# The last row of wo in two column parts, y copied 640 to 384, stores awaited on GpSimd, and wq loaded in 4, 2 and 2 blocks

## The chip, the cores and the metric

One core of a Trainium2 chip. The metric is device time in microseconds (us) of one execution; most executions of a kernel agree within 0.3%. "Fast" and "slow" are states of the chip. Ratios are the mean time of one kernel's fast runs over the mean of the other's fast runs of the same rounds, so they are not quite the ratio of the medians that are quoted beside them.

## The reference

Attention of four new tokens for each of 32 sequences over a cache of 2048 keys, with a projection ahead of it and one behind:

```python
B, Sq, D = 32, 4, 1024
Hq, Hkv, Sk, Dh = 32, 4, 2048, 128           # all arrays bf16
q = (x @ wq).reshape(B, Sq, Hq, Dh).transpose(0, 2, 1, 3)
k, v = repeat(k_cache, 8, axis=1), repeat(v_cache, 8, axis=1)
p = softmax(einsum("bhqd,bhkd->bhqk", q, k) * Dh ** -0.5)
y = einsum("bhqk,bhkd->bhqd", p, v).transpose(0, 2, 1, 3).reshape(B, Sq, Hq * Dh) @ wo
```

The k and v caches are 2 MB each for each sequence, wq and wo 8 MB each: 151 MB to be read.

## The kernel before

`big` in SBUF has eight slots of 2 MB. Slots 0 to 3 hold wq at first and v later (so the first four v loads wait for the projection, "qproj"); slots 4 to 6 hold k in turn. A k load waits until the transposes of the k that was in its slot three sequences earlier are done on VectorE (DVE). All loads go through one queue, issued by SyncE (SP) in program order.

```python
LEAD, S1, S2, VS, KS = 3, 6, 12, 4, 3
NC = D // 2
WO = (4, 4, 4, 4, 4, 4, 2, 2, 2, 1, 1)        # rows of wo (256 KB each) in each load
...
for c in range(4):                            # wq: four loads of 2 MB
    p.dma("sp", lambda e, c=c: e.dma_start(w_sb[:, 2*c:2*c+2, :], wq_v[:, 2*c:2*c+2, :]), [], ("wq", c), f"s_w{c}")

loads = [("k", b) for b in range(LEAD)]       # order: k0 k1 k2, v0 k3, v1 k4, v2 k5, ...
for b in range(B):
    ahead = b + LEAD + (b >= S2)
    ks = [("k", a) for a in range(len(loads) - b, ahead + 1) if a < B]
    loads += [("v", b)] + ks if b < S1 else ks + [("v", b)]
for kind, b in loads:
    waits = ["qproj"] * (b < VS) if kind == "v" else []
    if kind == "v" and b >= VS: waits = [("pv", b - VS)]
    if kind == "k" and b >= KS: waits = [("kt", b - KS, 1)]
    ...                                       # p.dma("sp", ... 2 MB into its slot)
...                                           # the loads of wo, in the pieces of WO
for kt in range(KT):                          # projection: 64 matmuls of 512 columns
    ... p.op("pe", mm, ["xT_evac", ("wq", kt // 2)], ...)
...
pe_idle(3, ring[0], xT_flat[:, 0:512], [("qs", 4)])   # keeps TensorE (PE) busy, then the transposes of q
...
def oproj(c):                                 # y = o @ wo, two matmuls of 512 columns for each row
    for h in range(sum(WO[:c]), sum(WO[:c + 1])):
        for j in range(2):
            ... p.op("pe", mm, [("wo", c), ("ot", B - 1)], ("op", j) if h == Hq - 1 else None)

def oproj_out():
    p.op("act", lambda e: e.activation(y_sb[:, 0:NC], ps_s[:, 0:NC], ACT.Copy), [("op", 0)], ("oe", 0))
    p.op("dve", lambda e: e.tensor_copy(y_sb[:, NC:D], ps_s[:, NC:D]), [("op", 1)], ("oe", 1))
    for j, eng in enumerate(("act", "sp")):   # each half is stored from its own queue
        p.dma(eng, ..., [("oe", j)], ("out", j), f"s_o{j}")
...
p.op("sp", lambda e: None, [("out", j) for j in range(2)])    # SP waits for both stores
```

## Time and profile before

| | before |
|---|---|
| median time, range (6 runs) | 363.35 us, 363.28 to 363.69 |
| span of the profiled run | 361.8 us (time 363.62) |
| read from HBM | 151.26 MB |
| first wo matmul that the end hangs on | 356.91 us |
| last landing of wo | 358.13 us |
| last landing of a store | 361.38 us |

How to read it: the span is the time from the first to the last instruction in the trace; the time of the execution is some 1.8 us longer. The lines of the profile that matter are shown and read in the prediction below, with the views they come from. "Landing" is the time at which a DMA engine reports its share of a load as done. A load is shared by 16 engines, so it has 16 landings, and what waits for the load waits for the last of them. The difference between the first and the last of the 16 is called the spread here.

### The profile page before, as it was taken

To read this page: it belongs to the slowest core of one execution; us is meant where nothing else is said; L and a number is where in the kernel's file an instruction comes from. 1 tells how busy PE (TensorE), PEld (TensorE's weight loads), DVE (VectorE), ACT (ScalarE), POOL (GpSimd) and SP (SyncE) were. 2 spreads that over 40 slices of the span, in tenths; PEclk is the share of its full clock that TensorE was granted. 3 is DMA by queue.
4 is the path that set the end of the run, shared out by engine and by line. 5 is a ranking of instruction groups with operands and counts; after the bars stand their busy time and mean duration, and the time that the engine had idled before them with its cause. 6 is when DMAs were issued, how large, how long until landed. Compare 5 with 4: busy or idle time off the path is not lost. (4 is left out here: it accounts for less than half of the span.)

```text
span 361.8 us, 6213 instructions
## 1 busy us (share of the span) xinstructions
PE 307.2 (85%) x3002; PEld 146.8 (41%) x2338; DVE 269.1 (74%) x170; ACT 102.8 (28%) x110; POOL 165.3 (46%) x262
## 2 busy tenths in 40 slices
PE   1988788999989999988999888888888889889896
PEld 1002000454444554444444444444333344449711
DVE  0018799999899888879998888888888888856500
ACT  1014222333333333333333333333322223333000
POOL 8002055355555555554455444445555554444000
PEclk9999999999999999999999999999999999999999
DMA  8999999999999999999999999999999999999995
GB/s 322 431 435 429 431 426 424 431 428 426 423 426 431 426 433 424 430 427 429 431 422 433 428 429 422 431 429 427 431 422 433 429 429 426 427 433 429 408 417 195
DMA packets 11819, 151.66 MB, mean 419 GB/s; under 512 B 1312, under 2 KB 1568, under 8 KB 2336
## 3 DMA queue, kind: packets, MB, share of 16 engines
q1 hardware_dynamic: 11664, 151.39, 98.7%
q8 instruction: 6, 0.10, 0.1%
q10 hardware_dynamic: 144, 0.13, 0.1%
q14 instruction: 5, 0.04, 0.0%
HBM read 151.26 MB, written 0.26 MB: 419 GB/s over the span
## 5 line engine op out<-in xcount | busy, mean ns | idle before, releaser
L325 DVE STREAM_TRANSPOSE KT_sb<-big 128x2048 f32<-128x2048 f32 x64 | 146.6, 2293 | 16.7 <-DMA big<-in_k_cache_dram 16.7
L351 ACT ACTIVATE P_sb<-ps_s,negmx 128x2048 bf16<-128x2048 f32 x32 | 82.1, 2565 | 185.0 <-DVE negmx L347 185.0
L16 PE MATMUL ps_s<-KT_sb,QD_sb 128*128 128x512 bf16 x384 | 103.7, 377 | 0.0
L382 POOL COPY PD_sb<-PT_sb 32x1024 f32<-32x1024 f32 x62 | 64.1, 1034 | 63.4 <-PE ps_r L391 60.5
L382 POOL COPY big<-PT_sb 32x1024 f32<-32x1024 f32 x61 | 63.0, 1034 | 59.1 <-PE ps_r L391 56.4
L347 DVE TENSOR_REDUCE negmx<-ps_s 128x1 f32<-128x2048 f32 x32 | 73.2, 2287 | 12.4 <-PE ps_s L16 11.0
L391 PE MATMUL ps_r<-big 128*128 128x128 bf16 x1024 | 59.8, 219 | 11.3 <-PEq L85 11.3
L391 PE MATMUL ps_r<-big,PD_sb 128*128 128x128 bf16 x1024 | 59.8, 219 | 9.9 <-PEq L85 9.9
L391 PEld LDWEIGHTS ps_r<-big 128*128 128x128 bf16 x1024 | 57.9, 98 | 22.1 <-issue 21.6
L391 PEld LDWEIGHTS ps_r<-big,PD_sb 128*128 128x128 bf16 x1024 | 58.0, 98 | 21.1 <-issue 20.6
L338 PE MATMUL ps_s<-KT_sb,QD_sb 128*128 128x512 bf16 x128 | 48.3, 377 | 18.4 <-PEq L85 18.4
L338 PEld LDWEIGHTS ps_s<-KT_sb,QD_sb 128*128 128x128 bf16 x128 | 12.4, 97 | 103.1 <-issue 103.1
L360 DVE STREAM_TRANSPOSE PT_sb<-P_sb 128x1024 f32<-128x1024 f32 x32 | 39.8, 1245 | 15.8 <-ACT P_sb L351 15.8
L315 POOL COPY QD_sb<-QT_sb 32x64 f32<-32x64 f32 x128 | 29.4, 229 | 46.2 <-DVE QT_sb L294 20.5
L16 PE MATMUL ps_r<-ident 128*128 128x384 bf16 x173 | 33.3, 325 | 0.0
L363 PEld LDWEIGHTS ps_r<-ssum,permf 128*128 128x128 f32 x64 | 11.9, 187 | 24.8 <-issue 23.1
L400 ACT ACTIVATE QT_sb<-ps_r,rinv 128x128 bf16<-128x128 f32 x32 | 11.7, 367 | 29.5 <-PE ps_r L391 27.3
L276 DVE TENSOR_SCALAR KT_sb<-ps_r 128x512 bf16<-128x512 f32 x2 | 1.3, 686 | 20.2 <-PE ps_r L260 20.2
L417 PE MATMUL ps_s<-big,KT_sb 128*128 128x512 bf16 x32 | 12.2, 380 | 2.2 <-DMA big<-in_wo_dram 1.4
L426 DVE CAST P_sb<-ps_s 128x512 bf16<-128x512 f32 x1 | 0.7, 692 | 16.1 <-PE ps_s L16 16.1
L16 PE MATMUL ps_s<-big,KT_sb 128*128 128x512 bf16 x32 | 12.1, 379 | 0.0
L249 PE MATMUL ps_r<-ident 128*128 128x384 bf16 x32 | 10.3, 323 | 0.0
(41 smaller groups left out, 85.1 us busy)
## 6 DMA issues: line engine op xcount, KB each, us to landing
big<-in_k_cache_dram SPq DMA_DIRECT2D x32, 2048.0 KB, 18.6
big<-in_v_cache_dram SPq DMA_DIRECT2D x32, 2048.0 KB, 22.0
big<-in_wq_dram SPq DMA_DIRECT2D x4, 2048.0 KB, 14.1
big<-in_wo_dram SPq DMA_DIRECT2D x6, 1024.0 KB, 22.8
big<-in_wo_dram SPq DMA_DIRECT2D x3, 512.0 KB, 24.5
big<-in_wo_dram SPq DMA_DIRECT2D x2, 256.0 KB, 21.0
P_sb<-in_x_dram SPq DMA_DIRECT2D x1, 256.0 KB, 2.7
out_dram<-P_sb ACTq DMA_DIRECT2D x1, 128.0 KB, 1.8
```

What stands on the lines that cost most here:

```text
L16: return eng.add_instruction(mybir.InstMatmult(name=nc.get_next_instruction_name(), engine=eng.engine, start_tensor_calc=start, stop_tenso ...
L315: p.op("pool", lambda e, s=src, d=dst: e.tensor_copy(d, s), waits if g == 0 else [("pt", i - 2)] * (g == 1 and i > 1), ("qd", i) if g == G ...
L325: p.op("dve", lambda e, s=src, d=dst: e.transpose(d, s), waits, ("kt", i, c), gives="t_kt" if c else None)
L338: mm = lambda e, a_=(out_, lhsT, rhs), f=first, l=last: e.matmul(a_[0], lhsT=a_[1], rhs=a_[2], start=f, stop=l, skip_group_check=True)
L347: p.op("dve", lambda e: e.tensor_reduce(negmx[:, i % 4:i % 4 + 1], ps_s[:, :], AX.X, ALU.max, negate=True), [("qk", i)], ("negmx", i))
L351: p.op("act", lambda e: e.activation(P_sb[:, :, :, :].rearrange("p t r w -> p t w r"), ps_s[:, :].rearrange("p (t w r) -> p t w r", w=2, r=R),
L360: p.op("dve", lambda e: e.transpose(dst, src), [("exp", i)], ("pt", i))
L363: p.op("pe", lambda e: e.matmul(ring[(i if i == L else i // 2 * 2) % 4][:, 510 + i % 2:511 + i % 2], lhsT=permf[:, :], rhs=ssum[:, i % 4:i ...
L382: p.op("dve" if i >= B - 2 and g < i - B + 4 else "pool", lambda e, s=src, d=dst: e.tensor_copy(d, s), [free] * (g == 0 or i >= B - 2) + [ ...
L391: p.op("pe", lambda e: e.matmul(buf[:, 0:Dh], lhsT=pd_of(i)[:, t // 2, :, :, :, t % 2].rearrange("p x g q -> p (x g q)"), rhs=big[:, slot_ ...
L400: p.op("act", lambda e: e.activation(dst, src, ACT.Copy, scale=rinv[:, i % 4:i % 4 + 1]), [("pv", i), ("rinv", i)], ("o", i))
L417: mm = lambda e, a=(out_, lhsT, rhs), h=h: e.matmul(a[0], lhsT=a[1], rhs=a[2], start=(h == 0), stop=(h == Hq - 1), skip_group_check=True)
```

## The change

Its intent: the end of the kernel should be shorter (the last row of wo is used in two parts as they land, the two copies of y take equally long, the sums lie so that the two copies read different PSUM banks, and SP has one wait less), and wq should come in three loads instead of four. The core of the diff:

```diff
-    NC = D // 2
-    WO = (4, 4, 4, 4, 4, 4, 2, 2, 2, 1, 1)
+    WO = (4, 4, 4, 4, 4, 4, 2, 2, 2, 1)
+    NA = 640
+    COLS = ((0, 0, 512), (512, 512, NA), (1024, NA, D))
+    WQ = (0, 4, 6, 8)
...
-        for c in range(4):
-            p.dma("sp", lambda e, c=c: e.dma_start(w_sb[:, 2 * c:2 * c + 2, :], wq_v[:, 2 * c:2 * c + 2, :]),
-                  [], ("wq", c), f"s_w{c}")
+        for c, (a, z) in enumerate(zip(WQ, WQ[1:])):
+            p.dma("sp", lambda e, a=a, z=z: e.dma_start(w_sb[:, a:z, :], wq_v[:, a:z, :]), [], ("wq", c), f"s_w{c}")
...
+        pieces = [(sum(WO[:c]), m, 0, D) for c, m in enumerate(WO)] + [(Hq - 1, 1, 0, NA), (Hq - 1, 1, NA, D)]
...
-                p.op("pe", mm, ["xT_evac", ("wq", kt // 2)],
+                p.op("pe", mm, ["xT_evac", ("wq", sum(kt >= z for z in WQ[1:]))],
...                                        # oproj: three matmuls a row, of 512, 128 and 384 columns
-            p.op("act", lambda e: e.activation(y_sb[:, 0:NC], ps_s[:, 0:NC], ACT.Copy), [("op", 0)], ("oe", 0))
-            p.op("dve", lambda e: e.tensor_copy(y_sb[:, NC:D], ps_s[:, NC:D]), [("op", 1)], ("oe", 1))
+            p.op("act", lambda e: e.activation(y_sb[:, 0:NA], ps_s[:, 0:NA], ACT.Copy), [("op", 1)], ("oe", 0))
+            p.op("dve", lambda e: e.tensor_copy(y_sb[:, NA:D], ps_s[:, 1024:1024 + D - NA]), [("op", 2)], ("oe", 1))
...
-        p.op("sp", lambda e: None, [("out", j) for j in range(2)])
+        p.ops["pool"].append((lambda e: None, tuple(("out", j) for j in range(2)), (), None))
```

More of the change, by code (lines that the diff above doesn't have):

```diff
@@ L216, in bass_standalone__gqa_block_cached__sampling_kernel @@
         wo_v = wo.rearrange("(h p e) n -> p h (e n)", p=128, e=4)
-        u0 = 0
-        for c, m in enumerate(WO):
-            assert u0 // 4 == (u0 + m - 1) // 4
-            kind, b = wo_for[u0 // 8]
-            dst, src = wo_at(u0, m), wo_v[:, u0 // 4, u0 % 4 * D:(u0 % 4 + m) * D]
+        pieces = [(sum(WO[:c]), m, 0, D) for c, m in enumerate(WO)] + [(Hq - 1, 1, 0, NA), (Hq - 1, 1, NA, D)]
+        assert sum(WO) == Hq - 1
+        for c, (u, m, n0, n1) in enumerate(pieces):
+            assert u // 4 == (u + m - 1) // 4
+            kind, b = wo_for[u // 8]
+            dst, src = wo_at(u, m), wo_v[:, u // 4, u % 4 * D:(u % 4 + m) * D]
+            if m == 1:
+                dst, src = dst[:, n0:n1], src[:, n0:n1]
             p.dma("sp", lambda e, dst=dst, src=src: e.dma_start(dst, src),
                 [("kt", b, 1) if kind == "k" else ("pv", b)], ("wo", c), f"s_wo{c}")
-            u0 += m
-        assert u0 == Hq
         p.op("pool", lambda e: e.memset(ident[:], 0.0), [], "ident0")
@@ L410, in oT_of, with oproj @@
             return oT_sb[:, u // 4, u % 4 // 2, :, :, u % 2].rearrange("p b s -> p (b s)")
-        def oproj(c):
-            for h in range(sum(WO[:c]), sum(WO[:c + 1])):
-                for j in range(2):
-                    out_, lhsT, rhs = ps_s[:, NC * j:NC * (j + 1)], oT_of(h), wo_at(h, 1)[:, NC * j:NC * (j + 1)]
-                    if j == 0:
-                        mm = lambda e, a=(out_, lhsT, rhs), h=h: e.matmul(
-                            a[0], lhsT=a[1], rhs=a[2], start=(h == 0), stop=(h == Hq - 1), skip_group_check=True)
-                    else:
-                        mm = lambda e, a=(out_, lhsT, rhs), h=h: _matmul_held(
-                            nc, e, *a, tile_size=(128, 128), tile_position=(0, 0), start=(h == 0), stop=(h == Hq - 1))
-                    p.op("pe", mm, [("wo", c), ("ot", B - 1)], ("op", j) if h == Hq - 1 else None)
+        def oproj(u):
+            for j, (at, n0, n1) in enumerate(COLS):
+                out_, lhsT, rhs = ps_s[:, at:at + n1 - n0], oT_of(u), wo_at(u, 1)[:, n0:n1]
+                if j == 0:
+                    mm = lambda e, a=(out_, lhsT, rhs): e.matmul(
+                        a[0], lhsT=a[1], rhs=a[2], start=(u == 0), stop=(u == Hq - 1), skip_group_check=True)
+                else:
+                    mm = lambda e, a=(out_, lhsT, rhs): _matmul_held(
+                        nc, e, *a, tile_size=(128, 128), tile_position=(0, 0), start=(u == 0), stop=(u == Hq - 1))
+                piece = next(c for c, (v, m, a, z) in enumerate(pieces) if v <= u < v + m and a <= n0 and n1 <= z)
+                p.op("pe", mm, [("wo", piece), ("ot", B - 1)], ("op", j) if u == Hq - 1 and j else None)
@@ L424, in oproj_out @@
         def oproj_out():
-            p.op("act", lambda e: e.activation(y_sb[:, 0:NC], ps_s[:, 0:NC], ACT.Copy), [("op", 0)], ("oe", 0))
-            p.op("dve", lambda e: e.tensor_copy(y_sb[:, NC:D], ps_s[:, NC:D]), [("op", 1)], ("oe", 1))
-            for j, eng in enumerate(("act", "sp")):
-                p.dma(eng, lambda e, j=j: e.dma_start(out_flat[:, NC * j:NC * (j + 1)], y_sb[:, NC * j:NC * (j + 1)]),
+            p.op("act", lambda e: e.activation(y_sb[:, 0:NA], ps_s[:, 0:NA], ACT.Copy), [("op", 1)], ("oe", 0))
@@ L429, in oproj_out @@
+            p.op("dve", lambda e: e.tensor_copy(y_sb[:, NA:D], ps_s[:, 1024:1024 + D - NA]), [("op", 2)], ("oe", 1))
+            for j, (eng, n0, n1) in enumerate((("act", 0, NA), ("sp", NA, D))):
+                p.dma(eng, lambda e, n0=n0, n1=n1: e.dma_start(out_flat[:, n0:n1], y_sb[:, n0:n1]),
                       [("oe", j)], ("out", j), f"s_o{j}")
@@ L474, in bass_standalone__gqa_block_cached__sampling_kernel @@
             o_turn(b0, n)
-        for c in range(len(WO)):
-            oproj(c)
+        for u in range(Hq):
+            oproj(u)
         oproj_out()
```

## The prediction

> **What bounds the kernel now.** I read four views: the page's slices, the chain of waits, the timelines of the start and of the last 5 us, and the loading queue's timeline. First the slices of the page:
>
> ```profile
> DMA  8999999999999999999999999999999999999995
> GB/s 322 431 435 429 431 426 424 431 428 426 423 426 431 426 433 424 430 427 429 431 422 433 428 429 422 431 429 427 431 422 433 429 429 426 427 433 429 408 417 195
> HBM read 151.26 MB, written 0.26 MB: 419 GB/s over the span
> ```
>
> The DMA engines are full in 38 of 40 slices, near 428 GB/s, and the bytes don't change. So a change can move the time in three places only: a gap in the stream of loads, a later finish of the slowest of the 16 engines, or the few us after the last byte of wo. The chain of waits agrees, its last third being a queued load of wo, then four rows of products, then the copy of y:
>
> ```profile
> 332.36 24.50 DMA big<-in_wo_dram
> 356.86 0.05 issue
> 356.91 0.39 PE ps_s L417
> ...
> 358.60 0.23 PE ps_s L16
> 358.82 0.02 issue
> 358.85 0.69 DVE P_sb L426
> ```
>
> The timeline of the end:
>
> ```profile
> 357.79 0.38 PE L417 MATMUL ps_s<-big,KT_sb 128*128 128x512 bf16 x1
> 358.00 0.38 PE L16 MATMUL ps_s<-big,KT_sb 128*128 128x512 bf16 x1
> 358.18 0.10 PEld L417 LDWEIGHTS ps_s<-big,KT_sb 128*128 128x128 bf16 x1 [0.51 <-DMA big<-in_wo_dram]
> 358.22 0.38 PE L417 MATMUL ps_s<-big,KT_sb 128*128 128x512 bf16 x1
> 358.43 0.38 PE L16 MATMUL ps_s<-big,KT_sb 128*128 128x512 bf16 x1
> 358.63 0.60 ACT L425 ACTIVATE P_sb<-ps_s 128x512 bf16<-128x512 f32 x1 [16.21 <-PE ps_s L417]
> 358.85 0.69 DVE L426 CAST P_sb<-ps_s 128x512 bf16<-128x512 f32 x1 [16.09 <-PE ps_s L16]
> 359.26 0.37 ACTq L428 DMA_DIRECT2D out_dram<-P_sb  x1
> 359.57 0.35 SPq L428 DMA_DIRECT2D out_dram<-P_sb  x1
> ```
>
> Two things are to be seen. The last row waits for its weights until 358.18, yet its matmul starts at 358.22, one regular pitch (0.216 us) after 358.00: the last load costs PE nothing. The wait that counts is that for rows 28 and 29 at 356.91; from there PE is the bound for four rows of 0.432 us. And ACT is done 0.31 us ahead of DVE, so the two stores are issued 0.31 us apart.
>
> The trace's packets and landings complete the end. The ACT store's packets start at 360.14; per engine it is eight packets of 1 KB, 46 ns each. The SP store's first packet starts at 360.51, when the first engine is through with the ACT store, and the last ends at 361.03; its completion is in at 361.38. SP then passes its wait at 361.40, its branch at 361.46 and its drain at 361.62, GpSimd opens the closing barrier at 361.65, and all is over at 361.84.
>
> **What the Trainium skill says.** "DMA: Bandwidth & Descriptors", section "Issuing engines are not separate DMA queues": transfers from different issuing engines run on the same 16 engines, and only issue time is saved. The trace agrees: the second store begins where the first ends. The same page, "Why small descriptors are slow": each packet carries a fixed overhead. The trace agrees: 4 KB takes 161 ns, 2 KB 84 and 1 KB 46, which is about 37.5 ns a KB plus 8.5. "TensorE: Matmul & The Clock Gate", section "What's actually happening": PE runs at half rate until it has been busy for a free-running window of some 3.4 us. The trace has a pitch of 427 ns from 8.79 on and 216 from 13.4. "PSUM — Partial Sum Buffer", section "PSUM bank collisions raise a hardware error": two engines must not touch one bank at once. No run here shows it, but it explains why the sums now lie in three banks: columns 0 to 639 in two for ACT, the other 384 in a third for DVE.
>
> **The change part by part.**
>
> *Last row in two loads (160 and 96 KB).* By the packet fit, eight packets of 1280 B and of 768 B take 8 x (55.4 + 36.6) = 736 ns an engine against 8 x 84 = 672, and one more 9 ns completion packet: the last landing moves from 358.13 to about 358.2. The first part lands near 357.95. PE starts the row at 358.22 by its own pitch in either case, and comes to the columns of the second part at 358.22 + 0.216 + 0.054 = 358.49. So nothing is gained or lost: 0.
>
> *Three matmuls a row (512, 128, 384).* The same 1024 columns; 216 + 54 + 162 ns. PE still ends at about 358.82. What ACT needs (512 + 128) ends at 358.49 + 0.163 of pipeline (0.379 - 0.216) = 358.65 against 358.60: +0.05.
>
> *Copies 640 and 384.* ACT: 597 ns for 512 columns. Rows of other widths give a slope of 0.60 ns a column (128 columns in 367 ns, L400) and 1.28 (2048 in 2565, L351, with scattered writes); I take 0.85 between them, an estimate, so 128 more cost 0.11: 0.70 us, from 358.69 to 359.39. DVE: 692 ns for 512 and 2287 for 2048 (L347) give 1.04 ns a column, so 128 fewer save 133: 0.56 us, from 358.85 to 359.41. Both stores are then issued at about 359.42 to 359.44: SP's 0.13 earlier, ACT's 0.16 later.
>
> *Stores.* This is the step that I hold to matter. The SP store was not limited by its issue but by the ACT store ahead of it on the same engines: 16 packets x 46 ns = 0.74 us of work on each engine, running without a hole from 360.14. Now the work is 8 x (55.4 + 36.6) = 0.74 us again, but it begins 0.88 us (the delay seen for ACT, 359.26 to 360.14) after 359.42, at 360.30. So the end moves by +0.16, unless two rings served in turn hide the 8.5 ns of each packet, which would give back up to 0.13. I take +0.10.
>
> *GpSimd waits instead of SP.* It removes one hop between engines (361.62 to 361.65, 0.03 us), but GpSimd now has its own two waits, branch and drain after the landing, where SP had them. -0.05 to +0.05; I take 0.
>
> *wq in 4, 2, 2.* PE starts when 4 MB have landed, at 13.6 and not at 8.8, and again cold. 64 matmuls: 3.4 to 6.8 us at 427 ns (the window is free-running), the rest at 216; worked out, the projection ends near 29.4 to 31 instead of 27.0, 2.4 to 4 us later. Does the stream see it? The loading queue's timeline:
>
> ```profile
> 27.03 0.33 SPq L209 DMA_DIRECT2D big<-in_v_cache_dram  x1
> 37.01 0.33 SPq L209 DMA_DIRECT2D big<-in_k_cache_dram  x1
> 44.95 0.33 SPq L209 DMA_DIRECT2D big<-in_k_cache_dram  x1
> ```
>
> The first v load waits for the projection; its data stream follows that of the third k load, which lands at 38.0, so 31 is early enough. The k load at 37.01 waits for the first K transposes and moves to 39.4 to 41; some 0.9 us later its packets can start, by 41.9, and the v load ahead of it is read until about 42.0 (its engines report between 42.39 and 42.90). The queue stays filled, just. The next at 44.95 has 7 us in hand. So 0, and one completion packet of 9 ns fewer.
>
> Sum: +0.10 us, and some -0.05 for what I may have priced too high at the barrier and in the packets: 363.6 us.
>
> **Rivals.** (a) The balanced copies do shorten the end: if the stores' overlap hides the packet overhead and the SP store ends with its own issue, the end is 0.13 earlier, and GpSimd's wait gives 0.05 more: 363.35. For it speaks that the copy on DVE is the last link of the chain; against it that the packets of the two stores abut. (b) The delayed projection opens a hole in the stream: if PE stays cold for longer than one window more, the k load comes after 42 and each us of delay is a us of time: up to 364.6. For it the margin of some 0.1 to 1.6 us; against it that the projection's delay has a ceiling. (c) The slowest DMA engine changes. In the landings all 16 engines are within 0.5 us until 53 us; then packets of instructions (16 KB on the page's queue 8) each set one engine back by about 1.5 us, and that engine lands last to the end (2.0 us of spread for every piece of wo). If 32 more PE matmuls called for another such packet, or another engine got one, the end would move by up to 0.5 either way. Against it: the last one was at 343.4, with some 200 PE instructions since the one before, and only about 92 were left then, 124 with the change.
>
> **Range and chances.** The known terms lie between -0.2 and +0.25 us; the three runs of before spread over 0.3. (b) and (c) give the longer tail above. 363.2 to 364.0 should hold it 8 times in 10. 2% would be 7.3 us, and nothing here is worth more than 1: same 0.985.
>
> **What would show it.** Right: PE's last matmuls end near 358.8, ACT's copy takes about 0.70 and DVE's 0.56 us, both stores are issued within 0.05 us of each other near 359.43, the first store packet is at 360.3, the last completion at 361.4 to 361.55; the k load of 37.01 is issued at 39 to 41 and the GB/s of the second to sixth slice stay near 430. Wrong: the last completion before 361.3 (rival a), a slice below 420 near 42 us (b), or the last wo landing off 358.2 by more than 0.3 (c).

## The result, and the profile after

| | before | after |
|---|---|---|
| median (6 runs each) | 363.35 us | 364.60 us |
| range | 363.28 to 363.69 | 363.52 to 365.38 |
| ratio of fast runs | | 1.0032, 95% interval 1.0015 to 1.0049 |

The change costs 0.3%: within 2% as forecast, but 1.0 us above the predicted 363.6 and outside its range. Two things are to be explained: 1.25 us of median, and a scatter of 1.9 us where before had 0.4.

The page's slices of the changed kernel:

```profile
GB/s 336 422 431 431 415 426 426 428 428 432 425 422 431 431 424 428 429 427 431 431 424 426 430 426 433 431 426 424 431 429 428 431 431 424 426 433 420 419 413 142
```

The second to sixth slice (9.1 us each) are the ones that the prediction named for its rival (b). The fifth holds 415 GB/s where before had 431, and from 36 to 45 us it is the stretch around 42 us. The loading queue's timeline of the changed kernel (start, length, engine, line, operation), to be held against the lines of before in the prediction (27.03, 37.01, 44.95):

```profile
30.16 0.33 SPq L210 DMA_DIRECT2D big<-in_v_cache_dram  x1
40.14 0.33 SPq L210 DMA_DIRECT2D big<-in_k_cache_dram  x1
40.51 0.43 SPq L210 DMA_DIRECT2D big<-in_v_cache_dram  x1
48.08 0.33 SPq L210 DMA_DIRECT2D big<-in_k_cache_dram  x1
```

Everything is 3.1 us later, as the prediction had it for a projection that starts late and cold. PE's timeline shows why: it starts at 13.54, when 4 MB have landed, and runs at the 427 ns pitch again (the times of a merged line cover three matmuls).

```profile
13.54 0.58 PE L262 MATMUL ps_r<-big,P_sb 128*128 128x512 bf16 x1 [9.04 <-DMA big<-in_wq_dram]
13.92 1.49 PE L16 MATMUL ps_r<-big,P_sb 128*128 128x512 bf16 x3
```

What the prediction did not have is what the load of 40.14 then meets. The trace does not name the engine of a packet; strung together by start and end into 16 chains, its packets run without a gap in before. In the changed kernel several engines have nothing to do between 41.8 and 43.2 us (called the hole below): the four longest gaps are 1.38, 0.60, 0.38 and 0.13 us, and the packets that follow take up to 1.08 us instead of 0.62. The load of 40.14 lands with a spread of 1.98 us (0.51 in before), its last engine 1.43 us later than in before and its first no later.

By itself this costs nothing for a long time: at 333.2 us both kernels have the same landing (333.26 before, 333.17 after), for in before too the last engine has fallen 2.0 us behind by then, through the instruction packets of the page's third part. Near 335.7 us another instruction packet of 16 KB comes. In before the next load's last landing follows after 4.89 us, the usual distance, so the packet fell to an engine that had time to spare. In the changed kernel it follows after 6.34 us: the packet fell to an engine that was last or nearly so. The spread goes from 2.07 to 3.48 us there, and stays above 3.3 to the last piece of wo. Whether this engine is the one that had the gap of 1.38 us is not shown; chains of packets cannot be followed over 300 us.

The late landing, that of the last v load at 339.51 (338.15 in before), has a second effect. PE's last products wait for it: L85 is the wait, and in both kernels it ends 0.03 us after this landing. Before first, then the change:

```profile
338.29 3.73 PE L391 MATMUL ps_r<-big 128*128 128x128 bf16 x64 [0.51 <-PEq L85]
```

```profile
339.64 5.36 PE L393 MATMUL ps_r<-big 128*128 128x128 bf16 x64 [1.97 <-PEq L85]
```

After the 1.97 us of idling the trace has PE's clock at half for 3.4 us (granted clock 0.69 over the stretch from 340 to 345 us), the same 64 matmuls take 5.36 us, and the products with wo begin at 346.11 instead of 342.91. The page's chain of the changed kernel therefore runs through PE, with short pieces of ACT and DVE, and not through a load of wo as in before:

```profile
PE 5%; DVE 0%; issue 0%; ACT 0%
```

The end of the changed kernel, in its timeline (the lines of before are in the prediction):

```profile
358.22 0.10 PEld L418 LDWEIGHTS ps_s<-big,KT_sb 128*128 128x128 bf16 x1 [0.67 <-DMA big<-in_wo_dram]
359.54 0.38 PE L418 MATMUL ps_s<-big,KT_sb 128*128 128x512 bf16 x1
359.76 0.38 PE L16 MATMUL ps_s<-big,KT_sb 128*128 128x128 bf16 x2
360.01 0.70 ACT L427 ACTIVATE P_sb<-ps_s 128x640 bf16<-128x640 f32 x1 [14.60 <-PE ps_s L16]
360.18 0.56 DVE L428 CAST P_sb<-ps_s 128x384 bf16<-128x384 f32 x1 [14.43 <-PE ps_s L16]
360.75 0.40 ACTq L430 DMA_DIRECT2D out_dram<-P_sb  x1
360.76 0.35 SPq L430 DMA_DIRECT2D out_dram<-P_sb  x1
```

The wait for rows 28 and 29 ends at 358.22 instead of 356.91, 1.31 us later. They landed at 358.18; by its own pitch PE would have come to them at 358.05. So in this execution the load decides, but by 0.18 us only: with these rows on time, the late PE alone would have kept 1.14 of the 1.31 us. Both are the work of late landings. What follows has the shape that the prediction gave it: copies of 0.70 and 0.56 us, both stores issued within 0.02 us. From 358.22 on, the span ends 5.09 us later; in before it ended 4.93 us after 356.91. So the end got longer by 0.16 us, not shorter.

### The profile page after: what moved, and what is told of

It reads as the page before. It is cut to its first block, busy times and chain, and to the rows that moved or that the text cites. A ratio compares the mean times of both kernels' runs of the same rounds, so it can differ in the third digit from the quotient of the medians.

```text
span 363.3 us, 6241 instructions
## 1 busy us (share of the span) xinstructions
PE 308.1 (85%) x3030; PEld 148.6 (41%) x2338; DVE 268.8 (74%) x170; ACT 103.0 (28%) x110; POOL 165.5 (46%) x262
## 5 line engine op out<-in xcount | busy, mean ns | idle before, releaser
L393 PE MATMUL ps_r<-big 128*128 128x128 bf16 x1024 | 61.4, 222 | 12.0 <-PEq L85 12.0
L393 PEld LDWEIGHTS ps_r<-big 128*128 128x128 bf16 x1024 | 59.6, 99 | 22.7 <-issue 22.3
L16 PE MATMUL ps_r<-ident 128*128 128x384 bf16 x173 | 33.3, 325 | 0.0
L16 PE MATMUL ps_s<-big,KT_sb 128*128 128x128 bf16 x64 | 12.2, 272 | 1.2 <-DVE KT_sb L409 1.1
L418 PE MATMUL ps_s<-big,KT_sb 128*128 128x512 bf16 x30 | 11.4, 379 | 0.0
L262 PE MATMUL ps_r<-big,P_sb 128*128 128x512 bf16 x8 | 3.5, 436 | 9.0 <-DMA big<-in_wq_dram 9.0
```

The source lines that it names most:

```text
L16: return eng.add_instruction(mybir.InstMatmult(name=nc.get_next_instruction_name(), engine=eng.engine, start_tensor_calc=start, stop_tenso ...
L393: p.op("pe", lambda e: e.matmul(buf[:, 0:Dh], lhsT=pd_of(i)[:, t // 2, :, :, :, t % 2].rearrange("p x g q -> p (x g q)"), rhs=big[:, slot_ ...
L418: mm = lambda e, a=(out_, lhsT, rhs): e.matmul(a[0], lhsT=a[1], rhs=a[2], start=(u == 0), stop=(u == Hq - 1), skip_group_check=True)
```

## The experiments

The theory: the time is the last engine's last landing of wo plus a fixed end. wq in 4, 2 and 2 makes the projection late, this makes one k load late, the queue runs dry near 42 us, and single engines fall behind by amounts that differ from run to run; the instruction packets add to whichever engine they meet. The first rival: the new end (copies, stores, GpSimd) is what costs. A second: the 32 KB packets of wq, or the late start of PE and DVE, do the harm in some way of their own.

The numbers of all runs are gathered here, from each profiled run's trace: when the first late k load (k3) was issued, the spread in its landing, the first and last engine at the last landing of wo, the time of that same execution, and that time less the last landing.

| kernel | k3 issued | spread there | wo: first / last engine | time | time less last |
|---|---|---|---|---|---|
| before | 37.01 | 0.51 | 356.16 / 358.13 | 363.62 | 5.49 |
| the change | 40.14 | 1.98 | 356.18 / 359.50 | 365.08 | 5.58 |
| after_again | 39.91 | 1.19 | 356.20 / 357.98 | 363.60 | 5.62 |
| tail_only | 36.87 | 0.32 | 356.18 / 357.82 | 363.41 | 5.59 |
| wq_only | 38.99 | 1.16 | 356.50 / 358.96 | 364.46 | 5.50 |
| after_v1first | 38.77 | 0.41 | 356.02 / 357.89 | 363.52 | 5.63 |
| late1 | 37.44 | 0.40 | 355.90 / 357.87 | 363.40 | 5.53 |
| late2 | 38.59 | 0.36 | 356.25 / 358.04 | 363.59 | 5.55 |
| late3 | 39.49 | 1.62 | 356.06 / 358.10 | 363.60 | 5.50 |
| late5 | 41.76 | 0.84 | 357.68 / 359.41 | 364.90 | 5.49 |
| late5_v1first | 41.39 | 0.41 | 356.02 / 358.09 | 363.59 | 5.50 |
| pool_only | 36.88 | 0.41 | 356.11 / 357.93 | 363.51 | 5.58 |
| best | 36.89 | 0.42 | 356.14 / 358.04 | 363.31 | 5.27 |
| best_again | 36.85 | 0.43 | 356.17 / 358.04 | 363.30 | 5.26 |

The last column carries the reading: it is 5.5 with the old end and the SP wait, 5.6 with the new end and in pool_only, 5.3 with the improved end, whatever the load stream did. All that varies beyond it in these traces is the last engine. Medians of before in the rounds of each group were 363.45 (tail_only to after_again), 363.45 (late3, late1, best, pool_only), 363.51 (late2, best_again) and 363.41 (late5 and its pair). Single runs of before at 365.02, 365.43 and 364.08 lie in these rounds and widen the intervals: only those of the first comparison and of late5 exclude 1. The single runs say more. Of before's 44 runs, 3 took 364.0 us or more; of the change's 11 it was 8, of late5's 4 all, of wq_only's 5 two, of late3's 4 two, of tail_only's 5 none, of after_v1first's 6 and late5_v1first's 4 one each.

**tail_only: the change without its wq part.**

```diff
-    WQ = (0, 4, 6, 8)
+    WQ = (0, 2, 4, 6, 8)
```

> The change without its wq part (wq again in four loads of 2 MB). Theory: the loss of 1.25 us comes from the later projection, which lets the queue of loads run dry near 42 us and leaves some DMA engines up to 2 us behind; a packet of instructions near 336 us then adds to one of them. So this kernel has no hole, its landings have the spread of before (2.0 to 2.1 us at the last wo piece), and it costs only the tail, +0.15 us: 363.4 to 363.6, with runs within 0.4 of each other. Rival (the tail is the cause: later stores, GpSimd's wait): it keeps the loss, 364.3 or more.

Measured: median 363.63 (363.41 to 363.81), ratio 1.0002 (0.9986 to 1.0018). No gaps near 42 us, spread of 1.64 us at the last wo piece, less than foreseen. Loss and scatter are gone in these five runs: the new end is not their cause. It costs up to 0.2 us, which the times alone don't separate from before.

**wq_only: the kernel before with wq in 4, 2 and 2.**

```diff
-        for c in range(4):                     # loads of 2 MB
+        for c, (a, z) in enumerate(zip((0, 4, 6), (4, 6, 8))):
```

> The kernel before with wq in loads of 4, 2 and 2 alone. Theory: the k load that before issued at 37.0 is issued near 40.1, there are idle stretches of some engines between 41.8 and 43.3, a spread of about 2 us in the next landing already, and runs that scatter by 1 us or more, median 363.8 to 364.8. Rival (tail): 363.3, like before. If the hole did nothing to the end by itself, at least one run in the six is as fast as before (363.3).

Measured: median 363.91 (363.65 to 364.46), ratio 1.0007 (0.9991 to 1.0024). The hole is there, though k3 came at 38.99 here: gaps up to 0.96 us, then packets of up to 1.60 us. The spread in k3's landing was 1.16, less than the 2 us expected, and all engines lost 0.3 us; instruction packets then made it 2.2 at 69 us and 2.5 at the end. No run was as fast as 363.3. Set against tail_only of the same rounds (363.41 to 363.81), the wq part brings the scatter and the larger loss; the ranges overlap, and it is the trace that makes the case.

**after_v1first: the whole change, but the second v load queued ahead of k3.** The second v load waits for the projection alone, so it can go out 10 us before k3.

```diff
             loads += [("v", b)] + ks if b < S1 else ks + [("v", b)]
+        i = loads.index(("k", LEAD))
+        assert loads[i + 1] == ("v", 1)
+        loads[i], loads[i + 1] = loads[i + 1], loads[i]
```

> The whole change, but the second v load (which needs only the projection) is queued ahead of the k load that comes late. wq stays in 4, 2 and 2 and its 32 KB packets stay. Theory: the projection is as late as in the change, but 2 MB (4.9 us) more are queued at 42 us, so no hole: 363.4 to 363.6 with little scatter. Rival (the 32 KB packets of wq, or the cold PE, do the harm themselves): 364.3 or more.

Measured: median 363.53; five runs from 363.47 to 363.59 and one at 365.06; ratio 1.0006 (0.9988 to 1.0025). The projection is late, wq has its 32 KB packets, and there is no gap. So neither is harmful by itself. The run at 365.06 has no trace. Its mean granted clock is 0.995, as in the change's profiled run, where PE spent 3.4 us at half clock; it may be the same, which is not shown. Before has such runs too, at a clock of 1.000, and what they are stays open.

**after_again: the change, unaltered.**

> The change, unaltered, for its scatter and a second trace. Theory: 363.5 to 365.4 again; in this trace some engines have idle stretches at 41.8 to 43.3 again, but perhaps other engines, so the spread at the last wo piece may be anything from 2.0 to 3.5 us, and the time is 363.4 plus what the spread has above 2.05. Rival (steady cost in the tail): little scatter and a spread of 2.0.

Measured: median 364.02 (363.60 to 364.46), ratio 1.0012 (0.9995 to 1.0029), in other rounds than the first comparison. The profiled run is one of the fastest, and its trace says why. The load is late again, and its first packets take up to 1.13 us, with hardly a gap (0.06 us) and a spread of 1.19 in its landing; but the instruction packet near 335.6 met an engine that was not behind, and the last spread is 1.77, less than the 2.0 to 3.5 expected. The same kernel thus gave 359.50 and 357.98 for the last landing, and times 1.48 us apart for 1.52 us of landing.

**late3, late1, late2: lateness alone.** The kernel before, wq in four loads, with the idle matmuls ahead of the transposes of q raised from 3 to 18, 9 and 14. Nothing but the time of the first K transposes, and so of k3, moves.

```diff
-        pe_idle(3, ring[0], xT_flat[:, 0:512], [("qs", 4)])
+        pe_idle(18, ring[0], xT_flat[:, 0:512], [("qs", 4)])     # late3; late1: 9, late2: 14
```

> The kernel before (wq in 2, 2, 2, 2; its own tail) with 15 more idle matmuls of 0.216 us between the projection and the transposes of q, so that the first K transposes, and the k load that waits for them, come about 2.6 us later: issued near 39.6 instead of 37.0. Theory (lateness of that load alone opens the hole): idle stretches or packets of 0.8 us and more at 41.8 to 44 us, a spread of 1 to 2 us in the landing that ends near 48 to 49, and a time of 363.4 to 365, scattered. Rival (the 32 KB packets or the cold start of PE): no hole, 363.4.

> The same with 6 more idle matmuls: the k load is issued near 37.7, some 4.2 us before the v load ahead of it is read. In the run with only wq changed, an issue 2.9 us before that point (38.99) still left engines idle to 42.8, 3.8 us after the issue. If that is the lead a load needs, this one is just early enough: a landing near 47.8 with a spread of 0.5, and 363.4. If the lead needed is more than 4.2 us, the spread there is over 0.7.

> The kernel before with 11 more idle matmuls ahead of the transposes of q: the k load is issued near 38.5, between late1 (37.44, no hole: spread 0.41 in its landing) and late3 (39.49, hole: 1.63). It is to bracket the lead that a load needs before the one ahead of it is read through (about 42.0). If the lead is near 3.0 us (some engines began 3.05 us after the issue in the change's trace): a small hole or none, spread 0.4 to 0.8. If it is nearer 4 us: spread 0.8 to 1.6 and scattered times of 363.5 to 364.3.

Measured: late3 363.82 (363.60 to 364.39), ratio 1.0010 (0.9986 to 1.0034); late1 363.44 (363.40 to 363.66), 0.9996 (0.9973 to 1.0019); late2 363.49 (363.38 to 363.59), 1.0000 (0.9984 to 1.0015). Stretches of 2 us of the profile show where the hole begins; in each line the stretch, its length, the busy times of PE, its weight loads, DVE, ACT and POOL, the clock, the DMA share and GB/s. Before, then late2, late3 and wq_only:

```profile
42.00:44.00 2.00, 0.17 (x1) 0.10 (x1) 1.58 (x2) 1.64 (x2) 0.00 (x0) 1.00 1.04 442
```

```profile
42.00:44.00 2.00, 1.54 (x10) 0.00 (x0) 2.00 (x2) 1.34 (x1) 0.00 (x0) 1.00 1.04 442
```

```profile
42.00:44.00 2.00, 2.00 (x15) 0.00 (x0) 2.00 (x2) 0.44 (x1) 0.00 (x0) 1.00 1.01 385
```

```profile
42.00:44.00 2.00, 1.94 (x12) 0.00 (x0) 2.00 (x2) 0.94 (x1) 0.00 (x0) 1.00 0.96 336
```

The last number is the one to read. The DMA share shows little of the hole: the packets after the gaps are longer, and count as busy throughout. With k3 issued at 38.59 the stretch is as full as in before; at 38.99 (wq_only) and 39.49 (late3) it is not. The number is no sure sign either: after_again has 434 there, with its long packets and its spread of 1.19. The v load ahead is read until about 42.0, so in these traces, one for each time of issue, a lead of 3.4 us was enough and one of 3.0 was not. In late3 the spread of 1.62 is not the hole's: an instruction packet at 41.4 had set one engine back by 1.2 us, and the v load ahead of k3 had landed with 1.63 already. Two other engines, at 0.94 and 1.31 (0.43 at most in the v load), are the hole's. That is why a clearer pair was run.

**late5 and late5_v1first: a large hole, and the same lateness without it.**

```diff
-        pe_idle(3, ring[0], xT_flat[:, 0:512], [("qs", 4)])
+        pe_idle(27, ring[0], xT_flat[:, 0:512], [("qs", 4)])     # late5; late5_v1first also swaps v1 and k3 as above
```

> The kernel before with 24 more idle matmuls ahead of the transposes of q: the k load comes near 41.4 us, later than in the change itself. In late3 a packet of instructions fell into the same stretch (41.4 us) and set one engine back by 1.2 us, so its spread was not the hole's alone; here the hole must be large enough to be seen past that. Theory: with the 3.0 to 3.4 us that a load needs, all engines run dry and resume at 43.5 to 45: under 300 GB/s between 42 and 44 us, the first engine of that load late by 1 us or more, and a median of 364.3 to 365.8. Rival (lateness itself is harmless, the 32 KB packets of wq did it): 363.5.

> late5 with the second v load queued ahead of the late k load, as in after_v1first. The projection, the K transposes and all that follows are as late as in late5, but 4.9 us more of loads are queued. Theory: no hole, near 430 GB/s between 42 and 44 us, 363.4 to 363.7. Rival (the late start of DVE and PE is itself what costs): the time of late5.

Measured: late5 364.85 (364.66 to 366.08), ratio 1.0045 (1.0022 to 1.0067); late5_v1first 363.56 (363.35 to 363.59, and one run at 365.22), ratio 1.0013 (0.9985 to 1.0040). The stretch from 42 to 44 us, late5 first:

```profile
42.00:44.00 2.00, 2.00 (x12) 0.19 (x2) 0.50 (x1) 0.00 (x0) 0.23 (x1) 1.00 0.83 164
```

```profile
42.00:44.00 2.00, 2.00 (x13) 0.10 (x1) 0.87 (x1) 0.00 (x0) 0.23 (x1) 1.00 1.12 475
```

Issued at 41.76, the load leaves all 16 engines without work; even the first one is 1.5 us later at the end (357.68), and the time is 1.4 us longer. With v1 ahead of it, k3 is nearly as late (41.39), and DVE and PE with it, but the stretch is full and nothing is lost at the end (gaps of up to 0.47 us come at 76.7 us and leave no mark on the last landing). The intervals of the two overlap through the run at 365.22; without a trace of it, the other three runs (363.35 to 363.59) and the last landings (359.41 and 358.09) decide. So the hole is the cause, not the lateness of the K transposes; and after_v1first excludes the late projection and the size of the packets.

**pool_only: the kernel before, with GpSimd waiting for the stores.**

```diff
-        p.op("sp", lambda e: None, [("out", j) for j in range(2)])
+        p.ops["pool"].append((lambda e: None, tuple(("out", j) for j in range(2)), (), None))
```

> The kernel before with GpSimd, not SP, waiting for the stores. From the last completion of a store to the end of the program: 0.456 us with SP in before, 0.44 us with GpSimd in the change's trace. Expected 0.42 to 0.46 us here, so no more than 0.03 us either way and 363.4. Rival (GpSimd's wake, branch and drain cost): 0.5 us or more.

Measured: median 363.48 (363.43 to 363.59), ratio 0.9996 (0.9972 to 1.0019). From the last store landing to the end 0.505 us, against 0.455 in before: a miss; GpSimd's wait costs 0.05 us here. In the change it took 0.444 us. There the store from ACT lands last, and its wait is the second of the two, so the first is already over.

**best and best_again: another end, with wq in 2, 2, 2, 2 and SP waiting.**

```diff
-    WO = (4, 4, 4, 4, 4, 4, 2, 2, 2, 1)
-    NA = 640
-    COLS = ((0, 0, 512), (512, 512, NA), (1024, NA, D))
-    WQ = (0, 4, 6, 8)
+    WO = (4, 4, 4, 4, 4, 4, 2, 2, 1, 1, 1)   # rows 28 and 29 in loads of their own
+    NA = 512                                 # last row in two halves, copies of 512 and 512
+    COLS = ((0, 0, NA), (512, NA, D))
+    WQ = (0, 2, 4, 6, 8)
```

> A version meant to beat both: wq in 2, 2, 2, 2, SP waiting; wo rows 28 and 29 in loads of their own; the last row in two halves of 512 columns, so that ACT's half is multiplied and copied while the second half lands; copies 512 and 512, stores as before. By the tail of before: the last row's first half starts at about 357.9 instead of 358.22, ACT's copy at 358.3 (was 358.63), DVE's at 358.65 (was 358.85), and the end follows ACT's store and DVE's copy: 0.2 to 0.3 us earlier from the last wo landing to the end (5.2 to 5.3 us instead of 5.5 between that landing and the time). Median 363.15 to 363.3. Rival (the tail is not on the path, only the engines' spread counts): 363.45.

> The improved version once more, unaltered, because one slow run of before (365.43, called fast) widened the interval of the first comparison. Median 363.1 to 363.35, 0.1 to 0.25 us under before in the same rounds; 3.46 us from the last wo landing to the end (3.70 in before, 3.81 in the change).

Measured: 363.29 (363.10 to 363.55), ratio 0.9990 (0.9973 to 1.0008), and 363.34 (363.23 to 363.40), ratio 0.9996 (0.9983 to 1.0010). The end in best's timeline:

```profile
357.76 0.10 PEld L418 LDWEIGHTS ps_s<-big,KT_sb 128*128 128x128 bf16 x1 [0.24 <-DMA big<-in_wo_dram]
357.87 0.38 PE L418 MATMUL ps_s<-big,KT_sb 128*128 128x512 bf16 x1
358.29 0.60 ACT L427 ACTIVATE P_sb<-ps_s 128x512 bf16<-128x512 f32 x1 [16.04 <-PE ps_s L418]
358.50 0.69 DVE L428 CAST P_sb<-ps_s 128x512 bf16<-128x512 f32 x1 [15.92 <-PE ps_s L16]
358.91 0.37 ACTq L430 DMA_DIRECT2D out_dram<-P_sb  x1
359.22 0.35 SPq L430 DMA_DIRECT2D out_dram<-P_sb  x1
```

The last landing of wo is at 358.04. ACT's copy begins 0.25 us after it, where before had 0.50, and the program ends 3.46 us after it (3.47 in best_again), where before had 3.70. The medians are 0.16 and 0.17 us below before in their rounds; the intervals include 1, so the times alone don't prove the gain; the traces show it.

## Why the prediction was wrong

**The step that failed** is the last of "wq in 4, 2, 2": "some 0.9 us later its packets can start, by 41.9, and the v load ahead of it is read until about 42.0 ... The queue stays filled, just." The issue was foreseen right for the change (39.4 to 41; 40.14 and 39.91 in its two traces; 38.99 and 38.77 in the two other kernels with the same wq), and so was the end of what was queued. The 0.9 us was wrong. It is the delay that the ACT store had on engines with nothing else to do. In the load stream, the last engine began 3.05 us after the issue (3.82 in wq_only); late2 and wq_only bracket the lead that was needed between 3.0 and 3.4 us. Against that, the issue at 40.14 left 1.9 us: where the prediction had a margin of 0.1 to 1.6 us, 1.1 to 1.5 us were missing. Why it takes so long stays open: in late5, where all engines had run dry, they began 0.96 to 1.70 us after the issue, and their first packets then took up to 1.69 us.

**Rival (b) was the right mechanism with the wrong law.** "Each us of delay is a us of time" fits only a hole that reaches all engines, as in late5 (1.5 us later on the first engine). A small hole sets single engines back, and up to some 1.5 us of that can be hidden (an estimate: before has one engine 2.0 us behind at the end and 0.5 ahead of the hole).

**Rival (c) was kept apart from it.** The prediction took an extra instruction packet as the danger. There was none: the page has the same six packets in both kernels.

```profile
q8 instruction: 6, 0.10, 0.1%
```

What differed was which engine was behind when one of them came. In the change's trace the spread went from 2.07 to 3.48 us at the packet near 335.7; in wq_only nothing happened there, and the next one, at 343.8, took it from 2.1 to 2.5; in after_again neither did harm. The "about 1.5 us" for each packet was too much for the first in before, which took the spread from 0.51 to 1.55. This part is read from three traces and not tested by an experiment that moves the packets. It fits the scatter, but how the hole picks its engines stays open.

**The range** was too narrow for this reason: the known terms were added, and rival (b), for which the margin was "some 0.1 to 1.6 us" on an untested delay, got almost no weight. Its own figure, up to 364.6, is the measured median, but by luck: the same kernel had 364.02 in the later rounds.

**What was right.** Both copies: 0.70 and 0.56 us. The two stores issued together: 0.02 us apart. The step "Stores": the packets of both stores take 0.90 us from the first start to the last end, as in before, so nothing of the packets' fixed cost is hidden, and the end moves with the start of the first store. From the landing of rows 28 and 29, the wait from which the prediction reckoned, to the end it is 4.98 us in the mean of the seven traces with the old end and SP's wait (4.97 to 4.99) and 5.13 in the four with the new one (5.12 to 5.14): +0.14 us. That is the +0.16 of the prediction without the hiding for which it took off 0.06. GpSimd's wait: between -0.01 and +0.05, predicted 0. The last row in two loads gained nothing: PE came to it at its own pitch, 359.54 in the trace, exactly three pitches of 0.434 after row 28 plus the first row's 0.01.

**The size.** In the rounds that had all four kernels, before was 363.45, the change 364.02, its wq part alone 363.91 and its end alone 363.63: +0.46 and +0.18 make +0.64 for the measured +0.57. In the rounds of the first comparison the change cost 1.25 us. The end costs the same in every trace, so the difference lies in the hole's part, whose size is a matter of chance.

## What to carry to other kernels

When a kernel is bound by its load stream, ask of every change ahead of it when the next load is issued and when what is queued will have been read; the needed lead is the delay measured in a running stream, here over 3 us in the traces that bracket it, not that of a transfer on idle engines. If a load will be late, queue one ahead of it that depends on something earlier, as after_v1first does. And look at the 16 landings of a load one by one: a bandwidth of 385 instead of 442 GB/s in one stretch of 2 us, and a DMA share of 0.97, were all that the stretches showed of the hole in the change. Last, follow a late landing to every engine that waits for it: here it also let PE idle, and its clock fell.

## What the Trainium skill lacked or had wrong

- "DMA: Bandwidth & Descriptors", section "Latency and other measured facts", gives a first-byte latency of about 600 ns for the hardware path that SP and ACT use, without saying from where it counts. From the start of the issuing instruction the traces have 0.88 us for a store and 1.0 us for the first load on idle engines; from its end, 0.51 and 0.63. The page does not give the lead that a load needs in a running stream: between 3.0 and 3.4 us in these traces, with the last engine starting 3.05 us after the issue in the change.
- "Runtime: NRT & Kernel Launch", section "Instruction fetch mechanics", says that instructions are fetched in blocks of 16 KB and that crossing a block is mostly hidden. The traces have packets of that size on the page's instruction queue (16384 bytes, 0.95 to 1.12 us each). In a load stream at its full rate such a block can set one DMA engine back by 1.0 us or more (the spread goes from 0.51 to 1.55 us at 56 us in before, and from 2.07 to 3.48 at 336 us in the change), and in these traces the stream does not make it up. The page does not say so.
- The pages looked up do not say that the engines of a load stream drift apart and stay so. In before the 16 landings of a load lie within 0.5 us until 53 us and 2.0 to 2.2 us apart from 74 us to the end.
